# Maxima by a repeated column, one group of norm products for W_out, and a new written-out order in a fused attention and MLP kernel

## The chip, the cores and the metric

One core of one Trainium2 chip runs the kernel. The metric is the device time of the whole program in microseconds, the median of several runs. Five engines run beside each other, each through its own queue in order: TensorE (PE in the profile, its weight loads PEld), VectorE (DVE), ScalarE (ACT), GpSimd (POOL), and SyncE (SP), which here issues nearly all DMAs.

## What is computed

```python
a = softmax(phi, axis=memory slots)                 # (8, 8, 576, 32)
k_m = einsum('bhsm,bhsd->bhmd', a, k); v_m = ...v   # 32 pooled keys and values a head
attn = softmax(q @ k_m^T / 8)                        # (8, 8, 576, 32)
x = (attn @ v_m), heads side by side                 # 4608 tokens x 512
h = x @ w_in                                         # 4608 x 2048
out = (h - tanh(h)) @ w_out                          # 4608 x 512, float32
```

The weights come as float64 and are read as pairs of 32-bit words. The kernel has a fast path for small h, which replaces h − tanh(h) by a polynomial; it is valid while the norms of v_m, of W_in's columns and of W_out's columns lie in windows that the kernel checks at run time. If the check failed, a second, general path would follow.

## The kernel before, in words

**Tiling and stages.** There are 8 batches (b) of attention and 18 units (u) of 256 tokens for the MLP, each unit in four blocks (fb) of 512 hidden columns. x is never formed: for each batch and block, P multiplies v_m by W_in (line 573), and the first product of the MLP, H (line 620), multiplies that by the attention weights. Every float32 operand that enters a product is split in a float16 high half and a low half, so a product is three.

**The order is written by hand.** `ORDER` (lines 71 to 133) is a list of words; `go` takes them one at a time, and each calls one step for the numbers behind it. A step that yields is continued by the next word of the same name: `H0.0 … H0.0` are the product and, later, its first reading on ACT. A trailing `x` turns around which PSUM place the step takes. `in_order` then chains all instructions of an engine in the order of the words, so the words fix the order on each engine (and in SP's DMA queue), while the engines wait for each other by data and by buffers alone. The words that matter here:

- `i…:tag`, `o…:tag`, `k…:tag`: SP loads a block of W_in, of W_out, or a block again for the check.
- `Z`: two warm-up products whose result nobody uses (line 856).
- `T`: float64 to float32 in three DVE steps (447, 450, 453), then ACT writes the high half (464). `L`, `Lv`, `Lp`: the low half by ACT and POOL (487, 489), by DVE (475), or by PE and ACT (481, 482, 484).
- `FX`, `FQ`: load the logits with tokens along the free axis. `X`: maxima of the logits over the tokens' axis of that layout (line 230 for batches 0 and 1, where they become the bias of an exponential, `YX`, line 235, and `XT`, `XU` turn the result on PE, 244 and 255, with copies 247 and 259; line 191 for the others). `XP`: the maxima of the other six batches, spread to all partitions by PE (202). `Y`, `YM`: subtract them; `YE`: exponential.
- `KA`, `KB`, `KR`: load k and v. `V`: pooling products (271, 279). `N`: divide (284, 285, 288). `U`, `UV`: turn and split the pooled k and v (311, 315, 545, 547).
- `Q`, `QT`: load q. `S`: scores (323) and their 32x32 transposes on DVE (332). `AM`, `AE`, `AD`, `AT`, `AS`: maximum, exponential, division, transposes back and split; their second halves run on POOL, or with a `v` on DVE.
- `P`: line 573, then a copy (586); `PL`, `PLp`: its low half on DVE (591) or by PE and ACT.
- `H`: line 620, then ACT squares it (627). `a`, `ap`: the polynomial on DVE, ACT, DVE (640, 642, 644). `g`, `c`/`cv`: high half on ACT (664), low half on POOL or DVE (670). `f`, `s`/`sv`: sums of blocks of it for a seven-product scheme (678 to 680), split on ACT (687) and POOL or DVE (691). `M`: the second product (748, or 767 for units 4 and later). `E`, `Ev`: the result is put together on DVE (806, 808, 817) and on POOL or, with a `v`, on DVE (810, 812), and stored.
- `SI`, `SO`: squares of W_in, W_out on ACT; `SS`, `SSv`: sums of them on POOL or DVE (508); `NI`, `NO`: column norms by products with a vector of ones (514, 529). `CW`, `CWv`: a window check of a weight block on ACT or DVE (498). `GG`, `GX`, `WD`: the verdict.

**The maxima before the change.** `top` takes the maximum per partition (two values), DVE multiplies them into two 128x128 diagonals (line 193), and `top_all` multiplies the 128x128 ones by these 256 columns in float32 (202), so that every partition has all 256 maxima.

**The norms of W_out before the change.** For each of four parts of four blocks: `SO` squares, `SS` sums four blocks to one 128x512 tile, `NO` makes four one-column products (529), ACT copies the four results (531); after the last part DVE sums the four parts (535).

Of the kernel before, what the change touches and what calls it, by code (L numbers as in the profile page):

```python
# [79 lines left out]
g2.0 M2.0 i12:kv2 T12 T12 T12 Y2 a2.1 CW1 H3.0 c2.0 T12 a2.1 Lv4 o11:gg T13 T13 P0.2 P0.2 M2.0 a2.1 H3.1 i14:kv3 g2.1 KA2 c2.1 ap3.0 FA3 PL0.2 YE2  # L80
Lv12 ap3.0 ap3.0 V2.0 V2.1 T6 P1.2x T13 M2.1 H3.1 M2.1 T6 T6 T13 g3.0 a3.1 N2 U2x P1.2 Lv13 PL1.2 a3.1 OP2 T6 OP2 UV2 T7 T7 T7 H0.2x H0.2 a3.1 g3.1 T7
Lv6 H1.2 H1.2 M3.0 c3.0 M3.0 a0.2 Lv7 ap1.2 a0.2 a0.2 P0.3 o12:kv2 T14 ap1.2 o14:kv3 Q2.1 BS0 U2 c3.1 g0.2 M3.1 M3.1 c0.2 P0.3 PL0.3 H1.3x ap1.2 T15
OP3 OP3 UV2 H0.3 T15 g1.2 H1.3 FQ3 c1.2 T15 H0.3 M0.2 T15 L15 a1.3 a1.3 S2.1 T14 T14 T14 S2.0x a0.3 a0.3 S2.1 S2.0 P1.3x P1.3 a1.3 g1.3 a0.3 P2.0 g0.3
AMv2.0 PL1.3 M0.2 L14 c1.3 c0.3 H2.2 H2.2 AMv2.0 AM2.1 AM2.1 a2.2 AE2.0 ADv2.0 P2.0 a2.2 H2.3 H2.3 a2.3 M1.2 M1.2 PL2.0 a2.2 BF0 g2.2 cv2.2 H3.2 L15
P2.1 H3.2 L14 M1.3 a2.3 a2.3 BH0 BL0 M1.3 ADv2.0 W2 AT2.0 ap3.2 P2.1 R1 O1 O1 AE2.1 ap3.2 ap3.2 PL2.1 BS1 BF1 AS2.0 AS2.0 M0.3 M0.3 H4.0 H4.0 ap4.0 R0
P2.2 H3.3 g2.3 c2.3 O0 O0 BH1 BL1 AD2.1 AD2.1 ap4.0 ap4.0 M2.2 R2 X3 g3.2 c3.2 P2.2 PL2.2 H3.3 H4.1 H4.1 ap3.3 ap3.3 g4.0 ap4.1 ap4.1 KR3.0 XP3 Y3
f4.0 s4.0 M2.2 QT3.0 ap3.3 g3.3 s4.0 YE3 cv4.0 M2.3 M2.3 H4.2 O2 O2 c3.3 ap4.1 AT2.1 R3 H4.2 BS2 P2.3 AS2.1 P2.3 g4.1 AS2.1 V3.0x PL2.3 ap4.2 ap4.2
BF2 BH2 M3.2 f4.1 ap4.2 f4.2 M3.2 H4.3x s4.1 KR3.1 s4.1 BL2 V3.1 N3 k4:q XX M3.3 M3.3 H4.3 ap4.3 ap4.3 g4.2 U3x U3 UV3 M4.0 M4.0 cv4.1 UV3 S3.0x ap4.3
O3 O3 P3.0 M4.0 M4.0 S3.0 AMv3.0 P3.0 M4.1 H5.0 BS3 AMv3.0 AE3.0 f4.3 k0:e g4.3 cv4.3 M4.1 M4.1 M4.1 PL3.0 c4.2 s4.2 s4.2 P3.1 H5.0 a5.0 a5.0 M4.2
sv4.3 H5.1 CW4 BF3 a5.0 BH3 BL3 H5.1 g5.0 k2:q c5.0 M4.2 M4.2 f5.0 QT3.1 M4.2 H5.2 s5.0 sv4.3 M4.3 P3.1 a5.1 ADv3.0 a5.1 M4.3 M4.3 PL3.1 S3.1 ADv3.0  # L90
s5.0 a5.1 AT3.0 M4.3 H5.2 S3.1 E4 g5.1 a5.2 a5.2 E4 CW2 f5.1 E4 E4 sv5.1 P3.2 M4.3 H5.3 H5.3 FQ4 M5.0 FA4 M5.0 a5.2 cv5.1 E4 E4 AS3.0 a5.3 sv5.1 M5.0
M5.0 CW0 AS3.0 H6.0 M5.1 M5.1 M5.1 M5.1 f5.2 a5.3 g5.2 KR4.0 cv5.2 s5.2 s5.2 a5.3 H6.0 a6.0 f5.3 a6.0 a6.0 P3.2 H6.1 s5.3 H6.1 f6.0 M5.2 M5.2 M5.2
M5.2 P3.3 g5.3 c5.3 s5.3 M5.3 ap6.1 ap6.1 PL3.2 H6.2 ap6.1 g6.1 P3.3 AM3.1 AM3.1 c6.1 AE3.1 X4 XP4 g6.0 M5.3 c6.0 s6.0 PL3.3 f6.1 H6.2 a6.2 KR4.1 M5.3
Ev5 Ev5 M5.3 s6.0 Ev5 Ev5 Ev5 a6.2 ADv3.1 ADv3.1 YM4 M5.3 s6.1 Ev5 a6.2 YM4 YE4 H6.3 H6.3 s6.1 QT4.0 AT3.1 ap6.3 ap6.3 M6.0 M6.0 AS3.1 AS3.1 g6.2 k3:e
f6.2 M6.0 sv6.2 V4.0 M6.1 M6.1 ap6.3 g6.3 f6.3 M6.0 M6.1 M6.1 sv6.3 sv6.2 H7.0 H7.0 a7.0 c6.2 V4.1 N4 W3 a7.0 sv6.3 M6.2 SI0 H7.1 a7.0 f7.0 H7.1 a7.1
U4 UV4 FQ5 UV4 M6.2 QT4.1 M6.2 a7.1 M6.2 U4 H7.2 H7.2 SSv0 NI0 a7.1 f7.1 a7.2 c6.3 M6.3 NI0 g7.0 a7.2 a7.2 s7.0 S4.0 c7.0 S4.0 AMv4.0 M6.3 M6.3 E6
s7.0 g7.2 c7.2 H7.3 H7.3 E6 a7.3 M6.3 E6 s7.1 E6 E6 W4 g7.1 M6.3 E6 s7.1 P4.0 P4.0 S4.1x S4.1 AMv4.1 a7.3 X5 CW3 AMv4.0 AE4.0 a7.3 g7.3 M7.0 M7.0 M7.0
M7.0 H8.0 H8.0 f7.2 c7.1 M7.1 M7.1 M7.1 M7.1 s7.2 f7.3 PL4.0 ap8.0 ap8.0 AMv4.1 AD4.0 ap8.0 XP5 s7.2 k5:e sv7.3 CW5 cv7.3 M7.2 KR5.0 AD4.0 f8.0 g8.0
M7.2 M7.2 M7.2 sv7.3 AE4.1 ADv4.1 s8.0 s8.0 c8.0 AT4.0 H8.1 YM5 ADv4.1 H8.1 P4.1 P4.1 M7.3 M7.3 a8.1 a8.1 a8.1 H8.2 AS4.0 PL4.1 M7.3 Ev7 H8.2 a8.2 FA5
QT5.0 YM5 a8.2 YE5 f8.1 M7.3 Ev7 P4.2 P4.2 g8.1 M7.3 AS4.0 c8.1 s8.1 s8.1 Ev7 Ev7 a8.2 g8.2 Ev7 H8.3 M8.0 Ev7 M8.0 c8.2 M8.0 V5.0 M8.1 AT4.1 AS4.1  # L100
KR5.1 PL4.2 H9.0 H8.3 a8.3 a8.3 a8.3 H9.0 f8.2 a9.0 a9.0 s8.2 s8.2 M8.1 M8.1 V5.1 f8.3 P4.3x P4.3 N5 s8.3 k6:e M8.0 M8.1 g8.3 H9.1x H9.1 a9.0 PL4.3
U5x s8.3 UV5 ap9.1 f9.0 M8.2 M8.2 UV5 ap9.1 ap9.1 c8.3 f9.1 M8.2 M8.2 M8.3 g9.0 c9.0 M8.3 SI1 k7:q SS1 U5 S5.0 g9.1 M8.3 sv9.0 k8:e E8 E8 H9.2 E8 E8
S5.0 M8.3 M8.3 AS4.1 H9.2 H9.3x sv9.0 CW6 ap9.2 ap9.2 ap9.2 QT5.1 c9.1 M9.0 M9.0 M9.0 E8 E8 s9.1 s9.1 AM5.0 H9.3 a9.3 AM5.0 f9.2 a9.3 FQ6 a9.3 NI1x
NI1 AE5.0 AD5.0 AD5.0 H10.0x H10.0 M9.1 M9.1 a10.0 s9.2 P5.0 f9.3 S5.1x a10.0 g9.2 P5.0 c9.2 a10.0 M9.0 M9.1 H10.1 s9.2 CW8 M9.1 M9.2 g9.3 c9.3 S5.1
AMv5.1 AMv5.1 AE5.1 M9.2 M9.2 M9.2 AT5.0 AS5.0 X6 XP6 s9.3 H10.1 s9.3 M9.3 PL5.0 ap10.1 H10.2 AS5.0 ADv5.1 ap10.1 ap10.1 g10.1 f10.1 g10.0 YM6 f10.0
H10.2 a10.2 FA6 P5.1 P5.1 c10.0 CW7 YM6 PL5.1 M9.3 a10.2 a10.2 QT6.0 M9.3 M9.3 M9.3 s10.0 E9 E9 s10.1 H10.3x KR6.0 H10.3 H11.0 cv10.1 a10.3 E9 E9 E9
E9 a10.3 a10.3 YE6 P5.2 P5.2 s10.0 M10.0 M10.0 M10.0 KR6.1 V6.0 H11.0 PL5.2 a11.0 H11.1 k10:q a11.0 s10.1 f10.2 s10.2 M10.0 M10.1 g10.2 a11.0 H11.1
ap11.1 f10.3 s10.2 ap11.1 M10.1 M10.1 ap11.1 f11.1 c10.2 M10.2 V6.1 N6 g10.3 c10.3 sv10.3 sv10.3 H11.2 SI2 SSv2 U6 UV6 U6 UV6 H11.2 a11.2 M10.2 M10.2
S6.0 QT6.1 ADv5.1 P5.3x a11.2 AT5.1 f11.0 P5.3 AS5.1 S6.0 M10.1 AM6.0 s11.1 PL5.3 AS5.1 a11.2 M10.3 M10.3 M10.3 E10 AM6.0 M10.3 s11.0 NI2 NI2 AE6.0
k9:e CWv9 s11.0 g11.0 E10 E10 H11.3 H11.3 E10 E10 AD6.0 g11.1 ap11.3 ap11.3 ap11.3 c11.0 g11.2 M10.2 M10.3 E10 H12.0x H12.0 a12.0 AD6.0 M11.0 c11.1  # L110
FQ7 AT6.0 a12.0 M11.0 M11.0 s11.1 M11.1 S6.1x c11.2 f11.2 S6.1 P6.0 M11.0 M11.1 M11.1 M11.1 k11:e f11.3 CW10 P6.0 PL6.0 X7 s11.2 s11.2 AS6.0 KR7.0
g11.3 c11.3 H12.1 P6.1 P6.1 a12.0 f12.0 H12.1 a12.1 s11.3 s11.3 M11.2 M11.2 M11.2 a12.1 PL6.1 a12.1 f12.1 M11.2 s12.0 g12.0 c12.0 H12.2 AS6.0 XP7 YM7
H12.2 a12.2 s12.0 M11.3 M11.3 M11.3 M11.3 FA7 a12.2 H12.3 g12.1 c12.1 Ev11 Ev11 H12.3 CWv11 a12.2 AM6.1 a12.3 a12.3 KR7.1 AM6.1 YM7 M12.0 Ev11 Ev11
Ev11 P6.2 a12.3 M11.3 H13.0 s12.1 s12.1 M12.0 M12.0 Ev11 M12.0 P6.2 PL6.2 g12.2 c12.2 H13.0 ap13.0 H13.1x M12.1 AE6.1 AD6.1 W5 ap13.0 ap13.0 M12.1
f12.2 QT7.0 M12.1 H13.1 YE7 a13.1 f13.0 sv12.2 sv12.2 g12.3 cv12.3 W6 a13.1 a13.1 V7.0 f12.3 H13.2 AD6.1 AT6.1 M12.2 M12.2 M12.2 QT7.1 M12.1 M12.2
# [1023 lines left out]
```

## Time and profile before

| | |
|---|---|
| median of 3 runs | 635.2 us (635.11 to 636.61) |
| the profiled execution | 635.34 us, span 633.1 us |
| granted TensorE clock | 0.998 |
| DMA | 85.03 MB, mean 134 GB/s |

The span is the time from the first to the last instruction of the profiled execution; what lies around it belongs to the time too. The profile's engines are busy in the sense of start to end of an instruction. Products on PE are pipelined: a product's listed duration holds its flight through the array, so the time from the start of one product to the start of the next is shorter than that duration, and it is the former that adds up.

### The profile page before, as it was taken

The page shows a single profiled execution, that of the slowest core. Times are in us where ns is not written, and L with a number is a line of the kernel's source. Part 1 is how long each engine was busy: PE and PEld are TensorE (multiplying, and loading weights), DVE is VectorE, ACT ScalarE, POOL GpSimd, SP SyncE. Part 2 cuts the span into 40 slices and gives each one's busy share as a digit, 9 for nine tenths or more (in the row PEclk, how much of TensorE's full clock was granted, in tenths as well). Part 3 has the DMA queues.
Part 4 walks back from the last instruction along what each step waited for, and adds up shares of the span by engine and source line. Part 5 has one row for each costly group of instructions (what it writes and reads, how often), then busy time and mean ns, then how long its engine had stood idle before and what let it go on. Part 6 is the DMA issues. An engine that isn't in the chain of part 4 may idle for free.

```text
span 633.1 us, 16291 instructions
## 1 busy us (share of the span) xinstructions
PE 618.6 (98%) x6908; PEld 485.4 (77%) x6908; DVE 570.4 (90%) x763; ACT 428.5 (68%) x601; POOL 350.7 (55%) x314
## 2 busy tenths in 40 slices
PE   8789999999999999999999999999999999999996
...
GB/s 342 415 290 281 245 248 179 97 73 68 188 136 159 51 75 66 64 163 120 108 96 110 120 60 154 105 88 173 38 38 172 119 102 84 50 152 35 167 100 39
DMA packets 25872, 85.03 MB, mean 134 GB/s; under 512 B 2752, under 2 KB 2752, under 8 KB 25024
## 3 DMA queue, kind: packets, MB, share of 16 engines
...
q8 instruction: 56, 0.92, 0.6%
...
HBM read 72.37 MB, written 11.53 MB: 133 GB/s over the span
## 4 chain that ended last, share of the span: by engine, by line
PE 83%; DVE 9%; DMA 4%; ACT 2%; issue 1%; SPq 0%; DVEq 0%; ACTq 0%
PE h L620 26%; PE x L767 22%; PE o L767 16%; PE o L748 7%; PE o1h L748 3%; PE pp L573 3%; DMA q<-in_qt_dram 2%; PE pkv L271 2%; DMA raw<-in_w_in_dram 2%; PE psc L323 1%; DVE h L640 1%; DVE h L644 1%; DVE bw L707 1%; DVE bw L700 1%; DVE s L678 1%
## 5 line engine op out<-in xcount | busy, mean ns | idle before, releaser
L620 PEld LDWEIGHTS <-ph 128*128 128x128 f16 x2304 | 178.2, 98 | 19.7 <-issue 4.0
L670 POOL TENSOR_TENSOR g<-h,g 128x512 f16<-128x512 f32 x114 | 128.3, 1147 | 100.1 <-ACT g L664 89.9
L691 POOL TENSOR_TENSOR f<-s,f 128x512 f16<-128x512 f32 x86 | 107.4, 1269 | 86.0 <-ACT f L687 81.1
L767 PEld LDWEIGHTS <-f 128*128 128x128 f16 x1344 | 129.2, 98 | 20.8 <-issue 5.2
L620 PE MATMUL h<-ah,ph 128*128 128x256 f16 (+3 forms) x1536 | 138.6, 246 | 0.7 <-DVE h L640 0.7
L767 PE MATMUL x<-bt,f 128*128 128x256 f16 x1008 | 128.3, 273 | 0.0
L642 ACT ACTIVATE u<-u,beta 128x1024 f32<-128x1024 f32 x72 | 82.5, 1146 | 46.7 <-DVE h L640 46.5
L767 PEld LDWEIGHTS <-g 128*128 128x128 f16 x1008 | 97.9, 98 | 14.7 <-issue 3.5
L627 ACT ACTIVATE u<-h 128x1024 f32<-128x1024 f32 x72 | 73.3, 1019 | 47.4 <-PE h L620 31.4
L640 DVE SCALAR_TENSOR_TENSOR h<-h,u 128x1024 f32<-128x1024 f32 x72 | 87.9, 1221 | 19.4 <-ACT u L627 17.9
L644 DVE SCALAR_TENSOR_TENSOR h<-u,h 128x1024 f32<-128x1024 f32 x72 | 92.7, 1289 | 11.7 <-ACT u L642 11.4
L664 ACT ACTIVATE g<-h 128x512 f16<-128x512 f32 (+2 forms) x128 | 68.2, 580 | 20.0 <-DVE h L644 13.4
L620 PE MATMUL h<-al,ph 128*128 128x256 f16 (+3 forms) x768 | 75.1, 246 | 0.0
L748 PEld LDWEIGHTS <-g 128*128 128x128 f16 x384 | 36.7, 98 | 45.2 <-issue 3.0
L687 ACT ACTIVATE f<-s 128x1024 f16<-128x1024 f32 x56 | 58.6, 1048 | 11.1 <-DVE s L680 7.0
L748 PE MATMUL o<-wout_hi,g 128*128 128x512 f16 x192 | 59.0, 379 | 0.0
L678 DVE TENSOR_TENSOR s<-h 128x512 f32<-128x512 f32 x56 | 45.3, 809 | 2.0 <-DVE h L644 0.5
L767 PE MATMUL o<-wout_hi,f 128*128 128x256 f16 x224 | 45.9, 273 | 0.0
L767 PE MATMUL o<-wout_hi,g 128*128 128x256 f16 x224 | 45.8, 273 | 0.0
L767 PE MATMUL x<-wout_hi,g 128*128 128x256 f16 x224 | 45.8, 273 | 0.0
L767 PE MATMUL o<-bt,g 128*128 128x256 f16 x336 | 45.3, 273 | 0.0
L586 ACT ACTIVATE ph<-pp 128x1024 f16<-128x1024 f32 x32 | 32.4, 1014 | 17.6 <-PE pp L573 16.7
...
## 6 DMA issues: line engine op xcount, KB each, us to landing
...
```

The lines of the kernel that those rows point to most:

```text
L620: nc.tensor.matmul(hp[:, k, tu : tu + w], st[b]["p"][fb][i][:, g, cs], st[b][ax][:, g, ta : ta + w], start=(n == 0 and k % 2 == 0 and m == ...
L627: nc.scalar.activation(uu, hp, AF.Square, scale=1.0 / (S_A * S_P))
L640: nc.vector.scalar_tensor_tensor(t, hp, C2 * S_G / (S_A * S_P), uu, op0=ALU.mult, op1=ALU.mult)
L642: nc.scalar.activation(uu, uu, AF.Square, bias=c["beta"])
L644: nc.vector.scalar_tensor_tensor(h3, uu, CC, t, op0=ALU.add, op1=ALU.mult)
L664: nc.scalar.activation(hi, x, AF.Copy)
L670: eng.tensor_tensor(lo[:, ks], x[:, ks], hi[:, ks], op=ALU.subtract)
L678: nc.vector.tensor_tensor(s[:, 0:2], pair, a_block(h3, 0, 0).unsqueeze(1).to_broadcast((P, 2, 2, P)), op=ALU.add)
L687: nc.scalar.activation(f[:, 0], s, AF.Copy)
L691: eng.tensor_tensor(f[:, 1, ks], s[:, ks], f[:, 0, ks], op=ALU.subtract)
L748: nc.tensor.matmul(o, gx[:, k, P * tt : P * tt + P], wx[:, 4 * fb + k, :], start=(first and k == 0 and wx is wout_hi and gx is gh), stop=( ...
L767: nc.tensor.matmul(dst, a(na, kk), b(nb, kk), start=(new and kk == 0 and na == 0 and nb == 0), stop=(end and kk == 1 and na == 1))
```

## The change

Three things. **One:** DVE no longer builds diagonals. PE takes the column of maxima, repeated 128 times by a stride of zero, as its stationary operand, and the identity as the moving one, once for each of the two columns. **Two:** the four parts' squares of W_out are added up in one float16 tile `wn` on POOL or DVE, and one group of four products and one copy on ACT follow; the window of that check is a little narrower. **Three:** `ORDER` is new. It has 1703 words for 1710 before: the words of the three norm groups are gone, and some steps go to another engine (`E` for `Ev` in units 5, 7, 11 and 14, `Lv2` for `L2`, and so on).

```diff
-WO_WIN = (1.002 * 2.0 ** -6, 3.493)
+WO_WIN = (1.004 * 2.0 ** -6, 3.486)
...
-        dg = big.tile([P, 2, P], F32, tag="qt", name=f"dg{b}", bufs=1)
-        nc.vector.tensor_tensor(
-            dg, self.c["ident"].unsqueeze(1).to_broadcast((P, 2, P)),
-            mx.unsqueeze(2).to_broadcast((P, 2, P)), op=ALU.mult,
-        )
-        d["dg"] = dg
+        d["mx"] = mx
...
-        nc.tensor.matmul(pa[:, 0, 0:256], self.c["ones"], dg.rearrange("p a b -> p (a b)"), start=True, stop=True)
+        for r in range(2):
+            row = d["mx"][:, r : r + 1].to_broadcast((P, P))
+            nc.tensor.matmul(pa[:, 0, P * r : P * r + P], row, self.c["ident"], start=True, stop=True)
...
     def squares_sum(i, eng=nc.gpsimd):
...
+        steps = [(0, 2), (1, 3)] if eng is nc.gpsimd else [(slice(0, 2), slice(2, 4))]
+        for k, m in steps:
             eng.tensor_tensor(sq[:, k], sq[:, k], sq[:, m], op=ALU.add)
+        if ("n", i) in acc:
+            if i == 0:
+                acc["n"] = big.tile([P, 512], F16, tag="wn", name="wn", bufs=1)
+            to = acc["n"] if i == 0 else sq[:, 0]
+            eng.tensor_tensor(to, sq[:, 0], sq[:, 1], op=ALU.add)
+            if i > 0:
+                eng.tensor_tensor(acc["n"], acc["n"], sq[:, 0], op=ALU.add)
+        else:
+            eng.tensor_tensor(sq[:, 0], sq[:, 0], sq[:, 1], op=ALU.add)
...
     def norms_out(part):
...
-            nc.tensor.matmul(pa[:, 0, k : k + 1], sq[:, 0, P * k : P * k + P], c["ones16"], start=True, stop=True)
-        yield
-        nc.scalar.activation(acc["n"][:, :, part], pa[:, 0, 0:4], AF.Copy, scale=(S_W * S_Q) ** -2)
-        yield
-        if part == 3:
-            o = N_CHECK - 4
-            nc.vector.tensor_reduce(stat[:, o : o + 4], acc["n"], axis=AX.X, op=ALU.add)
+            nc.tensor.matmul(pa[:, 0, k : k + 1], acc["n"][:, P * k : P * k + P], c["ones16"], start=True, stop=True)
+        yield
+        nc.scalar.activation(stat[:, N_CHECK - 4 : N_CHECK], pa[:, 0, 0:4], AF.Copy, scale=(S_W * S_Q) ** -2)
```

The start of the order, up to the first pooling of batch 1 (`V1.0`):

```diff
-Z0.0 i0:gg i1:gg T0 T0 T0 T0 Z0.0 Z0.0 Z0.0 Z0.0 Z0.0 i6:kv3 T3 T3 T3 Z0.0 Z0.0 Z0.0 Z0.0 Z0.0 FX0 T3 Z0.0 Z0.0 Z0.0 Z0.0 Z0.0 X0 Lp0 Lp0 YX0 Z0.0
-Z0.0 Lp3 Lp3 Z0.0 XT0 i2:gg i3:pp5 T1 T1 T1 i4:kv2 T1 XT0 XU0x T2 KA0 XU0 Z0.0 T2 T2 V0.0 Z0.0 Z0.0 Lv1 KB0 V0.1 N0 T2 L2 L2 U0x UV0 o2:gg Z0.0 Z0.0
-o3:gg Z0.0 T9 T9 T9 U0 Q0.0 S0.0x S0.0 Q0.1 S0.1 UV0 KA1 P0.0x P0.0 P0.1 PLp0.0 AM0.0 AM0.0 AE0.0 P0.1 PLp0.1 o4:gg o5:pp2 S0.1 AM0.1 AM0.1 AD0.0
-AD0.0 AE0.1 AD0.1 W0 AT0.0 T10 T9 AD0.1 AT0.1 PLp0.1 AS0.0 Q1.0 AS0.0 PLp0.0 Lp9 H0.0x ASv0.1 T10 ASv0.1 H1.0 Lp9 T10 T10 L10 o6:gg o7:gg H1.1 H0.0
-T11 T11 FX1 X1 o1:gg YX1 a0.0 o0:pp2 L10 H1.0 XT1 Z0.0 T11 T8 T8 T8 XT1 XU1 XU1 a1.0 a0.0 KB1 V1.0 a0.0 V1.1 T8 Lv8 a1.0 g0.0 H1.1 c0.0 N1 T11 L11
+i1:gg Z0.0 Z0.0 Z0.0 Z0.0 Z0.0 Z0.0 Z0.0 Z0.0 Z0.0 Z0.0 Z0.0 Z0.0 Z0.0 Z0.0 Z0.0 i0:gg T0 T0 FX0 X0 YX0 XT0x T0 T0 i6:kv3 T3 i2:gg i3:pp5 Lp0 Z0.0 T3
+T3 XT0 Z0.0 Z0.0 i4:kv2 T1 T3 Lp3x KA0 Lp3 XU0x XU0 V0.0 T1 T1 T2 KB0 T1 T2 T2 Lp0 o2:gg Lv1 o3:gg T2 Lv2 Z0.0 Z0.0 Z0.0 Z0.0 V0.1 N0 U0x T9 T9 T9 UV0
+Z0.0 Z0.0 Z0.0 U0 Q0.0 S0.0x S0.0 Q0.1 S0.1 T9 UV0 P0.0x P0.0 o5:pp2 o4:gg AM0.0 AM0.0 AE0.0 P0.1x P0.1 S0.1 AM0.1 o6:gg AM0.1 AE0.1 AD0.0 W0 PLp0.0
+PLp0.0 AD0.1 AD0.0 AT0.0 T10 PLp0.1 PLp0.1 AD0.1 AT0.1 o7:gg T10 Q1.1 Lp9 KA1 AS0.0 ASv0.1 AS0.0 H0.0x FX1 Lp9 H0.0 T10 ASv0.1 H1.0 T11 T11 T10 L10
+H1.0 L10 X1 o1:gg o0:pp2 H1.1 YX1 XT1 XU1 KB1 Z0.0 a0.0 a0.0 XT1 XU1 o9:pp4 T11 T11 T8 T8 T8 T8 a1.0 a1.0 o10:pp5 a0.0 L11 V1.0 g0.0 c0.0 V1.1 N1 Lv8
...
```

More of the change, by code (lines that the diff above doesn't have):

```diff
@@ L80 @@
[L80 to L115, printed above, removed]
```

84 lines of the change are left out of this document (58 added, 26 removed).

## The prediction

> **What bounds the kernel now.** I read the page first: span, engines, slices, chain.
>
> ```profile
> span 633.1 us, 16291 instructions
> ...
> PE 618.6 (98%) x6908; PEld 485.4 (77%) x6908; DVE 570.4 (90%) x763; ACT 428.5 (68%) x601; POOL 350.7 (55%) x314
> ...
> PE   8789999999999999999999999999999999999996
> ...
> PE 83%; DVE 9%; DMA 4%; ACT 2%; issue 1%; SPq 0%; DVEq 0%; ACTq 0%
> ```
>
> TensorE (PE) has 98% of the span and 83% of the chain that ended last. Its slices are full but for the first three and the last. So I asked for four stretches: up to the first k/v pooling of batch 0 (V0.0), up to that of batch 1 (V1.0), the body, and the tail.
>
> ```profile
> 0.00:19.40 19.40, 16.09 (x62) 7.28 (x62) 14.10 (x22) 8.94 (x11) 1.20 (x16) 1.00 0.92 357
> 19.40:48.00 28.60, 23.52 (x326) 14.81 (x330) 25.43 (x46) 18.47 (x28) 10.28 (x7) 1.00 0.89 345
> 48.00:628.00 580.00, 578.77 (x6528) 463.35 (x6520) 530.41 (x696) 401.06 (x563) 339.23 (x291) 1.00 0.34 117
> 628.00:633.10 5.10, 0.26 (x3) 0.00 (x0) 0.42 (x1) 0.00 (x0) 0.00 (x0) 0.73 0.33 116
> ```
>
> The columns after the length are the busy time of PE, its weight loads, DVE, ACT and POOL, then the clock, the DMA share and GB/s. In the body PE is idle for 580.00 − 578.77 = 1.23 us, and the view of its waits there has these two:
>
> ```profile
> PE h L620 <- DVE h L640: 0.7, 1, 0.7
> PE pkv L271 <- issue: 0.4, 1, 0.4
> ```
>
> This decides how the new order must be read. DVE at 530.41 of 580 us, ACT and POOL may be emptied or filled: while PE is never without work, that is worth nothing beyond the 1.23 us. What can shorten the kernel is PE work removed, or an earlier moment at which PE goes over to unbroken work (V1.0, 47.66). What can lengthen it is a later such moment, dearer PE work, or new waits in the body. The tail holds the last eviction and its store, in the same order after the change.
>
> **Part 1, the start of the order.** These rows of the timeline carry it:
>
> ```profile
> 6.33 0.43 DVE L447 TENSOR_SCALAR wt<-raw 128x512 uint32<-128x512 uint32 x1 [0.82 <-DMA raw<-in_w_in_dram]
> 6.67 1.28 DVE L450 SCALAR_TENSOR_TENSOR wt<-raw,wt 128x512 uint32<-128x512 uint32 x2
> 9.08 0.69 DVE L447 TENSOR_SCALAR wt<-raws 128x1024 uint32<-128x1024 uint32 x1
> 9.20 1.06 ACT L464 ACTIVATE win_hi<-wt 128x1024 f16<-128x1024 f32 x1 [7.18 <-DVE wt L453]
> 9.80 1.23 DVE L450 SCALAR_TENSOR_TENSOR wt<-raws,wt 128x1024 uint32<-128x1024 uint32 x1
> 10.71 1.02 PE L481 MATMUL pw<-wt,idw 128*128 128x512 f32 x2
> 12.20 1.35 DVE L230 TENSOR_REDUCE mx<-pt 128x2 f32<-128x1152 f32 x1
> 12.86 1.03 PE L856 MATMUL warm<-nid 128*128 128x512 f16 x4
> 13.29 1.00 ACT L484 ACTIVATE win_lo<-pw 128x1024 f16<-128x1024 f32 x1
> 14.19 1.43 ACT L235 ACTIVATE pt<-pt,mx 128x576 f32<-128x576 f32 x2
> 18.84 0.54 ACT L259 ACTIVATE e<-pkv 64x128 f32<-64x128 f32 x2
> 19.44 1.10 PE L271 MATMUL pkv<-kv,e 128*32 128x129 f32 x32 [1.42 <-ACT e L259]
> 20.47 1.04 PE L856 MATMUL warm<-nid 128*128 128x512 f16 x4
> 21.43 1.09 PE L271 MATMUL pkv<-kv,e 128*32 128x129 f32 x32
> 23.09 0.16 DVE L284 TENSOR_SCALAR kr<-pkv 128x2 f32<-128x2 f32 x1 [2.20 <-PE pkv L279]
> 23.89 0.87 DVE L447 TENSOR_SCALAR wt<-raw 128x512 uint32<-128x512 uint32 x2
> 26.35 0.72 PE L323 MATMUL psc<-q,kT 64*32 64x288 f32 x16 [0.70 <-DMA q<-in_qt_dram]
> 27.16 0.78 DVE L332 STREAM_TRANSPOSE sc<-psc 128x576 f32<-128x576 f32 x1
> 41.56 1.34 DVE L230 TENSOR_REDUCE mx<-pt 128x2 f32<-128x1152 f32 x1
> 47.66 1.98 PE L271 MATMUL pkv<-kv,e 128*32 128x129 f32 x64 [0.64 <-ACT e L259]
> ```
>
> Block i1 now lands first, so T0's first step waits for i0, at 6.33. Its L450 pair (1.28) ends near 8.3. X0, moved up, reduces for 1.35, to 9.6; its logits are the third transfer instead of the fourth. YX0's two exponentials (1.43) hold ACT to 11.1, and T0's conversion (1.06) stands behind them, to 12.1. PE then makes Lp0's product (2.15 us from the row at 10.71 to the next at 12.86), three warm words (0.43 each: two words fill 12.86 to 13.72), and Lp3's product from 15.6 to 17.7. T3's conversion doesn't hold that up: behind X0 come 1.28 + 0.69 + 1.23 and once more 1.23 on DVE and 1.06 on ACT, to 15.1. On ACT, Lp3's copy (1.00) is now ahead of XU0's two (0.54): they end at 19.5, and V0.0, which waits for them, starts at 19.5 instead of 19.44. Four steps were reordered, and nothing is won.
>
> Between V0.0 and V0.1 stand four warm words now, two before. Two words cost 21.43 − 20.47 = 0.96 with the switch to V0.1, so V0.1 starts at 19.5 + 1.03 + 1.83 = 22.36, which is **0.9 us later**. Queued behind it: N0 on DVE waits for V0.1 (23.09, behind 2.20 us of idleness; Lv2, which was POOL's and ACT's L2, goes into that gap). Behind N0 stand T9's three steps, from 23.89 right up to the transposes of S0.0 at 27.16. The q transfer that releases S0.0 at 26.35 doesn't move, so S0.0 stays, but its transposes slide to about 28.1. From there to X1 (41.56) DVE has the same steps as before, nearly without a gap, and X1 releases YX1, XT1, XU1 and V1.0 one after another. So V1.0 goes from 47.66 to 48.6, with the same PE work done ahead of it. T9's conversion, moved up on ACT, and H0.0's square, ahead of T10's, lie in ACT gaps; the order of the later loads changes, but FX1 still waits for AT0.1. Bounds: 0, if DVE catches up on the way (of its idle 28.60 − 25.43 = 3.17 us in that stretch, 2.20 lie ahead of N0, and 0.97 after it or elsewhere), to 1.9, if Lp9, which now waits for PLp0.0's copy on ACT, adds one copy (1.00) that lasts past V1.0. I take **+0.9**: what is left of DVE's idle time is waits for POOL and ACT inside the very chain that slides.
>
> **Part 2, the products.**
>
> ```profile
> L529 PE MATMUL pno<-ones,sqo 128*128 128x1 f16 x16 | 1.0, 165 | 0.0
> L202 PE MATMUL pmx<-dg,ones 128*128 128x256 f32 x12 | 3.7, 394 | 0.0
> L202 PEld LDWEIGHTS pmx<-dg,ones 128*128 128x128 f32 x12 | 1.8, 191 | 0.0
> L244 PE MATMUL pet<-ident,pt 128*128 128x128 f32 x16 | 2.3, 278 | 0.8 <-ACT pt L235 0.8
> L244 PEld LDWEIGHTS pet<-ident,pt 128*128 128x128 f32 x16 | 1.8, 140 | 1.4 <-ACT pt L235 1.2
> L193 DVE TENSOR_TENSOR dg<-ident,mx 128x256 f32<-128x256 f32 x6 | 3.4, 573 | 0.2
> ```
>
> Norms: four groups of four take 1.0 us, 0.25 each from first start to last end. The flight of the last (0.165) lies under what follows, which leaves 0.09. Three groups go: **−0.3**. The three evictions and the reduction that go are ACT's and DVE's, off the path. The added sums, one more on POOL or DVE for each later part, delay only NO3, which the check at the very end waits for.
>
> Maxima: six products of one 256-column stream in two passes (12 records) become six pairs of 128 columns (24 records). One of the old took 3.7 / 6 − 0.394 = 0.22 between its two starts, 0.44 in all. Four passes of half the columns are 0.44 again if the stream sets the pace, as it does in the transposes: 1.04 us for eight less their flight is 0.11 each, although their loads are listed at 140 ns. If the load of a two-pass fp32 product (191 ns, the row of the product that is replaced) sets the pace, a pair takes 0.76, that is +0.33, and six +2.0. Below nothing it can't go, the columns being as many. Nearest is the transposes' row, of the same shape, but its loads are shorter; I take 0.1 each, **+0.6**. The 573 ns that DVE saves are no PE time.
>
> [...]
>
> **Part 3, the moved steps of the body.** Net, DVE gives four evictions' adds to POOL, and three windows to ACT; it takes four of the attention's splits, three of the low halves of g and one of f, and loses the six L193 products. All of that lies beside PE's 578.77 us. The steps that stand just in time before a product are about as many as before, and each such place can become a wait. Bounds: −1.2, if both old waits go, to about +4, if the body's start became as loose as the stretch before it (28.60 − 23.52 = 5.1 us idle). I take 0, nearest to the body's own row.
>
> Sum on the profiled execution (635.34 us, span 633.1 and 2.2 around it): +0.9 − 0.3 + 0.6 + 0 = +1.2, so 636.5. It ran 0.14 above the median of 635.2; by the median I forecast **636.4**. A difference under 0.3% (1.9 us) counts as none, since that is about what a measurement here can tell.
>
> **Rivals.**
> *Hidden anyway* (12%): DVE catches up the 0.9 us before X1, and the maxima stream like transposes. Only −0.3 stays: 634.9. For it: the 0.97 us of idle DVE. Against: waits inside a chain slide with it.
> *The maxima's loads set the pace* (14%): 635.2 + 0.9 − 0.3 + 2.0 = 637.8, slower. It decides from 0.22 us a product on (1.3 us for six). For it: 191 ns against a stream of 0.11; against: 140 against 0.11 did no harm.
> *New waits in the body* (17%): some 2 to 4 us where just-in-time steps come late, 638.4 to 640.4. For it: 1.23 us of waiting leaves far more room to get worse than better. Against: DVE's sum is smaller.
> *A shorter start* (12%): the T9 conversion (1.06) that leaves ACT's queue ahead of PLp0.1 brings V1.0 forward by as much, and the body loses its waits: 635.2 − 1.06 − 0.3 − 1.23 = 632.6, faster. Against: X1's chain on DVE, not ACT, ends last there.
>
> **How the numbers follow.** The forecast has 45%. Some 5% of it lies over 637.1, so slower is 14 + 17 + 5 = 36%, same 40 + 12 = 52%, faster 12%. The range leaves out the shorter start and the upper end of the new waits: 633.7 to 639.6.
>
> **What would show it.** V1.0 near 48.6 in the timeline, V0.1 near 22.4 and the S0.0 transposes near 28.1 show part 1 right; V1.0 at 47.7 or sooner refutes it. Part 2: the pairs of maxima between 0.44 and 0.76 us from start to the next work, and one group of norms at L529's successor. Part 3: PE idle between V1.0 and the tail near 1.2 us. If it is over 3 us, or V1.0 comes a microsecond sooner, the forecast is wrong.

## The result and the profile after

The changed kernel takes **640.18 us** (median of 4 runs, 639.89 to 640.76), the kernel before 635.51 beside it: 1.0072 times as long, interval 1.006 to 1.0084. The forecast was 636.4, its range ended at 639.6. The page of the profiled execution (640.17 us):

```profile
span 638.1 us, 16280 instructions
...
PE 620.1 (97%) x6908; PEld 486.2 (76%) x6908; DVE 565.4 (89%) x756; ACT 433.3 (68%) x607; POOL 348.1 (55%) x313
...
PE   8789999999999999999999999999999999999995
...
PE 71%; DVE 19%; ACT 5%; issue 2%; POOL 2%; DMA 0%; SPq 0%; DVEq 0%; POOLq 0%; ACTq 0%
```

PE's slices look as before; the chain does not: DVE had 9% of it and has 19% now, although DVE is busy for 5.0 us less. The four stretches, cut where V0.0, V1.0 and the tail begin:

```profile
0.00:19.40 19.40, 16.13 (x59) 7.18 (x59) 13.03 (x21) 7.25 (x10) 1.20 (x16) 1.00 0.91 350
19.40:48.20 28.80, 23.98 (x319) 14.64 (x320) 27.25 (x47) 20.28 (x30) 8.18 (x6) 1.00 0.91 350
48.20:630.80 582.60, 579.71 (x6531) 464.35 (x6532) 524.72 (x689) 405.79 (x569) 338.75 (x291) 1.00 0.34 116
630.80:638.10 7.30, 0.27 (x3) 0.00 (x0) 0.42 (x1) 0.00 (x0) 0.00 (x0) 0.83 0.24 84
```

PE's idle time in the body is 582.60 − 579.71 = 2.89 us (1.23 before), the tail 7.30 us (5.10 before), V1.0 at 48.2 (47.66 before). The view of PE's waits in the body (engine, line, what it waited for; us in all, times, longest) had two rows before; now:

```profile
PE pp L573 <- DVE ph L591: 0.8, 1, 0.8
PE pp L573 <- DVE h L640: 0.4, 1, 0.4
PE pkv L268 <- ACT e L223: 0.4, 1, 0.4
PE pkv L268 <- PE h L620: 0.4, 1, 0.4
PE pp L573 <- DVE h L644: 0.3, 1, 0.3
PE h L620 <- DVE ph L591: 0.3, 1, 0.3
```

Four of the six, 1.8 of 2.6 us, are waits for a place in PSUM that DVE (the cubic's L640 and L644, the low halves' L591) has not yet read out. For V7.0 and V3.0 (`pkv`) the view names another engine, but both start 0.10 us behind the end of a step of the cubic on DVE (473.23 and 179.35). The view counts from the modelled end of a product's flight. Counted from start to start against what the same word takes elsewhere in the trace, nine words lose 4.42 us: P4.2 0.96, P5.2 0.60, P3.0 0.55, V7.0 0.55, V3.0 0.52, H5.1 0.44, P3.2 0.34, H5.0 0.26, H6.0 0.20. Before it was three: H5.2 0.84, V5.0 0.58, P5.2 0.30, in all 1.72.

In the start, the timeline shows V0.0, V0.1, N0, S0.0's transposes, X1 and V1.0:

```profile
19.39 1.09 PE L268 MATMUL pkv<-kv,e 128*32 128x129 f32 x32 [1.33 <-ACT e L256]
...
22.25 0.82 PEld L268 LDWEIGHTS pkv<-kv,e 128*32 128x32 f32 x32 [0.42 <-issue]
...
23.83 0.16 DVE L281 TENSOR_SCALAR kr<-pkv 128x2 f32<-128x2 f32 x1 [0.16 <-PE pkv L276]
...
27.71 0.77 DVE L329 STREAM_TRANSPOSE sc<-psc 128x576 f32<-128x576 f32 x1
...
42.11 1.33 DVE L227 TENSOR_REDUCE mx<-pt 128x2 f32<-128x1152 f32 x1
...
48.19 1.07 PE L268 MATMUL pkv<-kv,e 128*32 128x129 f32 x29 [0.21 <-ACT e L256]
```

So the span's 5.0 us are: start +0.53, V1.0 to the first product of the last word (M17.3) 582.06 in place of 579.78 (+2.28), last product to the end +2.19 (the tails go by the span as printed and are good to 0.05 us). In what follows "start" is V1.0, "body" and "tail" are these two lengths (the last word's six products between take 0.55).

My theory then: the order makes the body's waits, the tail is a code effect, the start is little. Rivals: the new products or sums cost the time; the tail belongs to the stores or the last words' order; the waits are local and can be filled.

### The profile page after: what moved, and what is told of

It is laid out like the page before. It is cut to its first block, busy times and chain, and to the rows that moved or that the text cites. A ratio compares the mean times of both kernels' runs of the same rounds, so it can differ in the third digit from the quotient of the medians.

```text
span 638.1 us, 16280 instructions
## 1 busy us (share of the span) xinstructions
PE 620.1 (97%) x6908; PEld 486.2 (76%) x6908; DVE 565.4 (89%) x756; ACT 433.3 (68%) x607; POOL 348.1 (55%) x313
## 4 chain that ended last, share of the span: by engine, by line
PE 71%; DVE 19%; ACT 5%; issue 2%; POOL 2%; DMA 0%; SPq 0%; DVEq 0%; POOLq 0%; ACTq 0%
PE h L620 21%; PE x L767 18%; PE o L767 14%; PE o L748 5%; DVE h L640 3%; DVE h L644 2%; PE pp L573 2%; PE pkv L268 2%; PE warm L856 2%; PE o1h L748 2%; DVE bw L707 1%; DVE ph L591 1%; DVE bw L700 1%; PE psc L320 1%; DVE s L678 1%
## 5 line engine op out<-in xcount | busy, mean ns | idle before, releaser
L670 POOL TENSOR_TENSOR g<-h,g 128x512 f16<-128x512 f32 x108 | 127.0, 1198 | 81.0 <-ACT g L664 76.7
L691 POOL TENSOR_TENSOR f<-s,f 128x512 f16<-128x512 f32 x84 | 102.8, 1244 | 93.8 <-ACT f L687 65.7
L644 DVE SCALAR_TENSOR_TENSOR h<-u,h 128x1024 f32<-128x1024 f32 x72 | 90.0, 1250 | 17.7 <-ACT u L642 14.6
L640 DVE SCALAR_TENSOR_TENSOR h<-h,u 128x1024 f32<-128x1024 f32 x72 | 87.7, 1220 | 15.1 <-ACT u L627 13.5
L678 DVE TENSOR_TENSOR s<-h 128x512 f32<-128x512 f32 x56 | 45.5, 812 | 1.6
L591 DVE SCALAR_TENSOR_TENSOR ph<-pp,ph 128x1024 f16<-128x1024 f32 x30 | 36.3, 1212 | 2.9 <-ACT ph L586 2.9
```

The lines of the kernel that those rows point to most:

```text
L640: nc.vector.scalar_tensor_tensor(t, hp, C2 * S_G / (S_A * S_P), uu, op0=ALU.mult, op1=ALU.mult)
L644: nc.vector.scalar_tensor_tensor(h3, uu, CC, t, op0=ALU.add, op1=ALU.mult)
L670: eng.tensor_tensor(lo[:, ks], x[:, ks], hi[:, ks], op=ALU.subtract)
L678: nc.vector.tensor_tensor(s[:, 0:2], pair, a_block(h3, 0, 0).unsqueeze(1).to_broadcast((P, 2, 2, P)), op=ALU.add)
L691: eng.tensor_tensor(f[:, 1, ks], s[:, ks], f[:, 0, ks], op=ALU.subtract)
```

## The experiments

All stages by the profile (span, V1.0, body, tail in us; time is the median, or the one run where there was one):

| run | span | V1.0 | body | tail | time | ratio to before, interval |
|---|---|---|---|---|---|---|
| before | 633.1 | 47.66 | 579.78 | 5.11 | 635.5 to 635.8 | |
| after | 638.1 | 48.19 | 582.06 | 7.30 | 640.18 | 1.0072 (1.006 to 1.0084) |
| e1_old_order | 635.8 | 48.26 | 581.83 | 5.17 | 637.11 | 1.0019 (1.001 to 1.0028) |
| e2_pad | 635.9 | 48.09 | 582.07 | 5.19 | 638.18 | 1.0039 (1.0025 to 1.0053) |
| e3_pad_before | 636.1 | 48.20 | 580.01 | 7.34 | 637.89 | 1.0035 (1.0021 to 1.0048) |
| e4_quarter | 643.7 | 47.69 | 588.0 | 7.5 | 645.8, one run | |
| e5_old_engines | 723.6 | 47.73 | 669.84 | 5.48 | 725.62 | 1.1419 (1.1402 to 1.1436) |
| e6_six_moved | 637.6 | 47.83 | 582.27 | 6.96 | 640.40 | 1.0073 (1.006 to 1.0087) |
| e8_two_warm | 638.1 | 48.10 | 582.15 | 7.30 | 640.20, one run | |
| e9_att4 | 639.8 | 48.24 | 583.36 | 7.65 | 641.99, one run | |
| e10_sum_later | 638.2 | 47.52 | 584.99 | 5.15 | 638.36 | 1.0041 (1.0027 to 1.0055) |
| e11_half_step | 634.6 | 48.12 | 580.32 | 5.61 | 636.96, one run | |
| e12_sum_idle | 636.1 | 47.68 | 582.69 | 5.18 | 638.24 | 1.0048 (1.0035 to 1.0062) |
| e13_fewer_warm | 636.5 | 47.63 | 583.11 | 5.22 | 638.26 | 1.0042 (1.0029 to 1.0055) |
| f1_maxima_only | 633.0 | 47.60 | 579.64 | 5.22 | 635.42 | 0.9998 (0.9989 to 1.0007) |
| f3_maxima_moved | 632.5 | 48.00 | 578.79 | 5.16 | 634.75 | 0.9982 (0.9973 to 0.9991) |
| f4_half_act | 638.6 | 47.99 | 582.56 | 7.51 | 640.67, one run | |
| f5_half_both | 634.2 | 48.31 | 579.73 | 5.61 | 636.70, one run | |

**The tail: e2_pad and e3_pad_before.** In both kernels ScalarE issues the last store, then branches over the second path. Before, its first instruction behind the branch is at 632.26 and the next at 632.34; after, the first is at 634.96 and the next only at 637.23, and every other engine waits for it at the closing barrier. In the trace, 769 instructions stand ahead of that branch in ScalarE's queue before and 782 after, so the code behind it lies elsewhere. That its place is what counts is the "code theory". The edit, with 4 copies in the changed kernel and 12 in the one before:

```diff
+    gap = const.tile([P, 1], F32, name="gap")
+    for _ in range(4):
+        nc.scalar.activation(gap, c["one"], AF.Copy)
     with ExitStack() as inner:
         split_path(inner, tc, c, ins, out)
```

> The changed kernel with four copies of one column added on ScalarE ahead of its first work, so that the code behind its last branch lies four instructions later. If the 2.2 us more in the tail are a wait for one more block of ScalarE's code: last product to end of span falls from 7.3 to about 5.1 and the time from 640.2 to 638.0, with no other stage moved by more than 0.2. If they belong to the stores or to the order of the last words: 640.2, tail 7.3.

> The kernel before with twelve such copies on ScalarE, which puts the code behind its last branch where the changed kernel has it. If the place of the code is what counts: the tail grows from 5.1 to about 7.3 and the time from 635.5 to 637.7. If it belongs to the changed order: 635.5, tail 5.1.

Both came as the code theory had it: 7.30 fell to 5.19, and 5.11 grew to 7.34; 638.18 and 637.89 us. All 18 profiles fit: the tail is 6.96 to 7.65 us in the seven runs where 781 or 782 instructions stand ahead of the branch, and 5.1 to 5.6 us where there are 766 to 777, or 786 (e2). In e6, with 781, the wait stands one instruction further on (634.86 to 637.23). In e11 and f5 there are 777, so their tails of 5.61 us are part of what they gain below.

In the trace ScalarE's branch is at 632.04 and the first instruction behind it at 634.96, 2.9 us later (629.23 and 632.26 before, 3.0). What the second wait, 2.2 us more, is for stays open. That it is a wait for one more block of code, the "if" of e2's expectation, is not shown: of the 8 KB packets of code (`instruction` among the profile's DMA queues) behind the last store, the sixth is over at 635.93 and the seventh begins at 637.87, when the wait is past.

**The code in the old order: e1_old_order, f1_maxima_only.** The order of before, less the words of three norm groups; then the kernel before with the maxima's edit alone.

> Both changes of the code (maxima as two products of a repeated column, one group of norm products) in the order of before; the three groups of norm words go. If the new order is what costs the time: 635.5 - 0.3 = 635.2 us, V1.0 within 0.2 of 47.7, six words of maxima at 0.44 each, last product to end of span about 5.1. If the pairs of maxima cost what the prediction took (0.1 each): 635.8. If the code is what costs the time (waits that follow from the products): 638 or more.

> The kernel before with the change of the maxima alone. If the pairs stream at 0.44 us and the six products that DVE loses (0.57 each) shorten the wait at V5.0 (0.58 to about 0.25): 635.6 - 0.3 = 635.3 us. If the pairs cost 0.1 each as the prediction took: 636.2. If the maxima cost the 1.4 us that the kernel with both changes in the old order lost: 637.

The six pairs take 0.44 to 0.53 us to the next product, the single products took 0.43 to 0.52: the maxima cost nothing. f1 is level with before (0.9998), with V5.0's wait down from 0.58 to 0.25 and one of 0.25 at V7.0 that was not there; so the 2.2 us between the bodies of f1 and e1 (1.3 to 1.7 us between their times) are the norms' change. e1 itself, 637.11, lies between what was expected of the order and of the code: its body, 581.83, is nearly as long as the changed kernel's 582.06, but its waits lie elsewhere. In e1 four words between 528 and 560 us lose 2.5 us, 1.49 of them before M15.0. The timeline there, in the kernel before and in e1, DVE's rows first and then GpSimd's, has the last of the sums (L508; L513), the forms of window 15.1 (L678 to L680) and GpSimd's step beside them:

```profile
548.20 1.14 DVE L508 TENSOR_TENSOR sqo<-sqo 128x1024 f16<-128x1024 f16 x2
549.25 0.68 DVE L678 TENSOR_TENSOR s<-h 128x512 f32<-128x512 f32 x1
549.97 0.43 DVE L679 TENSOR_TENSOR s<-s,h 128x256 f32<-128x256 f32 x1
550.43 0.42 DVE L680 TENSOR_TENSOR s<-s,h 128x256 f32<-128x256 f32 x1
...
550.65 1.34 POOL L564 TENSOR_TENSOR al<-af,ah 128x576 f16<-128x576 f32 x1 [2.61 <-ACT ah L562]
```

```profile
550.28 0.42 DVE L513 TENSOR_TENSOR wn<-wn,sqo 128x512 f16<-128x512 f16 x1
550.62 0.68 DVE L678 TENSOR_TENSOR s<-h 128x512 f32<-128x512 f32 x1
551.34 0.42 DVE L679 TENSOR_TENSOR s<-s,h 128x256 f32<-128x256 f32 x1
551.80 1.39 DVE L680 TENSOR_TENSOR s<-s,h 128x256 f32<-128x256 f32 x1
...
553.56 0.42 DVE L808 SCALAR_TENSOR_TENSOR r<-x,r 128x256 f32<-128x256 f32 x1
...
551.56 1.35 POOL L564 TENSOR_TENSOR al<-af,ah 128x576 f16<-128x576 f32 x1 [2.61 <-ACT ah L562]
```

One added step of 0.42 us puts L680 behind the start of GpSimd's L564 in place of ahead of it, and L680 takes 1.39 in place of 0.42: it ends 0.28 us behind GpSimd's step. L808, two steps further on in DVE's queue, then ends at 553.98, and M15.0, which by the view of waits waited for it, starts at 554.13:

```profile
PE x L767 <- DVE r L808: 1.3, 1, 1.3
```

**The same sum elsewhere: e10_sum_later, e12_sum_idle, e13_fewer_warm.**

From e1's order, `SSv2` moves from behind `k24:q` to behind the third `a15.2` (e10) or behind `f15.2` (e12, e13), and e13 also drops three of the first sixteen `Z0.0`. For e12:

```diff
-k24:q SSv2 M14.3 M14.3 AS7.1
+k24:q M14.3 M14.3 AS7.1
...
-f15.2 s15.2 a15.3
+f15.2 SSv2 s15.2 a15.3
```

> The order of before with both changes of the code, the third sum of W_out's squares (DVE) moved behind the last step of window 15.2. If the added 0.42 us step, put ahead of window 15.1, made M14.1 to M15.0 wait in the kernel with the old order: the 2.5 us lost there go, 637.1 - 2.5 = 634.6 us, under the kernel before by the three groups of norm products (0.3) and part of the wait at V5.0. If the sums cost as much wherever they stand: 637.

> The order of before with both changes of the code, the third sum of W_out's squares moved to where GpSimd is idle for 3 us (behind the step f15.2). If its steps on DVE are short (0.68, 0.42, 0.42) only while GpSimd is idle, the 2.5 us lost at M14.1 to M15.0 mostly go: 634.6 to 635.2 us, the kernel before at 635.75. If any place in that stretch is too full for 1.5 us more: 637 or more.

> As e12, without three of the sixteen warm words that stand ahead of PE's first real product (they compute nothing that is used). Where the full clock is granted late (7.4 us), that product waits for the warm words until 11.5 us, but its operand is there at 10.3: if so, V0.0 comes at 19.0 to 19.5 whatever the moment, V1.0 at 47.5 to 47.7, 0.3 to 0.6 us less than e12. If the start hangs on the transfers instead: as e12.

Both places failed: 638.36 and 638.24. The profiled execution of e10, 640.08, is the slowest of its five: behind a wait of 3.25 us for DVE's L817, which stands behind the long sums, the clock was granted at half for 3.41 us, so its body of 584.99 lies some 1.7 us above what the median stands for. The durations are as e12 expected, though. The three steps in e10, beside a busy GpSimd, and in e12, beside an idle one:

```profile
553.90 1.64 DVE L506 TENSOR_TENSOR sqo<-sqo 128x1024 f16<-128x1024 f16 x1
555.57 1.26 DVE L511 TENSOR_TENSOR sqo<-sqo 128x512 f16<-128x512 f16 x1
556.87 1.26 DVE L513 TENSOR_TENSOR wn<-wn,sqo 128x512 f16<-128x512 f16 x1
```

```profile
559.34 0.68 DVE L506 TENSOR_TENSOR sqo<-sqo 128x1024 f16<-128x1024 f16 x1
560.06 0.43 DVE L511 TENSOR_TENSOR sqo<-sqo 128x512 f16<-128x512 f16 x1
560.52 0.43 DVE L513 TENSOR_TENSOR wn<-wn,sqo 128x512 f16<-128x512 f16 x1
```

The three take 4.2 us beside the busy GpSimd and 1.5 beside the idle one. In e12 the waits of 1.49 and 0.40 us from M15.0 on are gone (those of 0.38 and 0.26 before it stay), but the short sums push DVE's next steps into GpSimd's (DVE's L644 begins at 560.86, GpSimd's L691 at 560.93), and H16.1, NO3 and H16.2 lose 2.1 us. Neither place had room for 1.5 us on DVE. e13 brought V0.0 to 19.18 us, but V1.0 stays at 47.63 (47.68 in e12) and H0.1 and U1 wait 0.5 us more: nothing won.

**The start: e8_two_warm.** `Lv2 Z Z Z Z V0.1 N0` becomes `Lv2 Z Z V0.1 Z Z N0`.

> The changed kernel with two of the four warm words between V0.0 and V0.1 put behind V0.1. As the prediction has it: V0.1 comes about 0.9 sooner after V0.0 (2.86 falls to 2.0) and the S0.0 transposes and V1.0 follow by about as much, V1.0 minus V0.0 from 28.8 to about 28. If other waits between (Lp9, XU1) take it up: V1.0 minus V0.0 stays within 0.2 of 28.8.

V0.1 comes 2.03 us behind V0.0 (2.86 in after), yet V1.0 stays at 48.10, now 29.12 us behind V0.0, which neither expectation had. DVE's rows in e8:

```profile
23.98 0.41 DVE L444 TENSOR_SCALAR wt<-raw 128x512 uint32<-128x512 uint32 x1
24.83 0.43 DVE L444 TENSOR_SCALAR wt<-raw 128x512 uint32<-128x512 uint32 x1 [0.44 <-DMA raw<-in_w_out_dram]
...
27.61 0.77 DVE L329 STREAM_TRANSPOSE sc<-psc 128x576 f32<-128x576 f32 x1
```

Here T9's second step waits for its transfer until 24.83, so the transposes are at 27.61 (27.71 in after). In after, DVE waits 0.16 us for V0.1's result and not for the transfer. So in this one execution the transfer takes what the two words gave.

Something else differs from profile to profile, whatever the order: the moment at which PE gets its full clock. PE's warm words begin at 1.94 in all runs, a product every 0.43 us until the full clock is granted and every 0.22 from then on. The stretch 4.90 to 7.90 (PE's products in brackets) in before, e1 and after:

```profile
4.90:7.90 3.00, 3.00 (x13) 1.27 (x12) 2.00 (x5) 0.00 (x0) 0.00 (x0) 1.00 1.02 414
```

```profile
4.90:7.90 3.00, 3.00 (x10) 1.15 (x9) 1.97 (x4) 0.00 (x0) 0.00 (x0) 1.00 1.03 416
```

```profile
4.90:7.90 3.00, 3.00 (x9) 1.15 (x8) 1.98 (x5) 0.25 (x1) 0.00 (x0) 1.00 1.02 404
```

The clock's column says 1.00 throughout, since the records begin with the first grant; the number of products tells the rate. By these records full rate begins at 5.73, 7.37 and 7.62. In the old order the first real products stand behind these words: V0.0 is at 19.44 and 20.26, V1.0 at 47.66 and 48.26, with the same words. The profile of before had an early moment, that of after a late one. At like moments (7.3 to 7.5) V1.0 is at 48.20 and 48.26 in the old order (e3, e1) and at 48.09 and 48.12 in the new (e2, e11); at 5.0 to 6.2, it is at 47.5 to 47.7 in the old and at 47.7 in the new (e4, e5), but at 48.3 in f5, where T9's second step waits for its transfer as in e8. So at like moments the two starts differ by some 0.1 us. The chain of part 1 is there all the same: in 16 of the 18 profiles V1.0 stands 25.9 to 26.4 us behind V0.1 (26.23 before, 25.94 after, 26.00 in e3), and the other two are e8 (27.09) and f5 (26.58).

**The maxima: e4_quarter.** Each pair cut into eight products of 32 columns.

```diff
-    nc.tensor.matmul(pa[:, 0, P * r : P * r + P], row, self.c["ident"], start=True, stop=True)
+    for q in range(0, P, 32):
+        nc.tensor.matmul(pa[:, 0, P * r + q : P * r + q + 32], row, self.c["ident"][:, q : q + 32], start=True, stop=True)
```

> The changed kernel with each pair of maxima cut into eight products of 32 columns (16 passes, each with its own load of the repeated column), the same columns in all. If the stream sets the pace: a word of maxima stays at 0.44 us. If each load of 0.19 us sets it: 16 x 0.19 = 3.0 us a word. If a load takes PE for the 0.11 us that 128 columns stream: 16 x 0.11 = 1.75.

```profile
L200 PE MATMUL pmx<-ident,mx 128*128 128x32 f32 x96 | 11.4, 272 | 0.0
L200 PEld LDWEIGHTS pmx<-ident,mx 128*128 128x128 f32 x96 | 11.3, 190 | 0.2
```

A word takes 1.70 to 1.79 us to the next product. Its sixteen passes start (11.4 / 6 − 0.272) / 15 = 0.109 us apart although every load is listed at 190 ns: in this run a pass with its float32 load takes PE 0.109 us, and the rest of the load's listed time lies beside other passes. A pass of the pairs, with 128 columns, takes no longer (0.44 us for four, 0.11 each; the old ones, with 256 columns, took 0.22), so there the loads add nothing.

**The body: e6_six_moved.** Six waiting words are moved behind the next ready product, for instance:

```diff
-M7.3 P4.2 s8.0 H8.2 M7.3 M7.3 c8.0
+M7.3 s8.0 H8.2 M7.3 M7.3 P4.2 c8.0
-V7.0 M12.1 a13.1
+M12.1 V7.0 a13.1
```

> The changed kernel with six words moved behind the next ready product (V3.0x, H5.1x, P3.2, P4.2, P5.2, V7.0), which lost 3.4 us between them waiting for a place in PSUM to be read out. If these waits are local: 640.2 - 3.4 = 636.8, at least 2.5 of it in the trace. If DVE sets the pace of the body and the waits come back at later words: within 1 us of 640.2.

The moved words wait no more, and the body is 582.27, no shorter (582.06 in after). The waits of e6:

```profile
PE h L620 <- DVE h L640: 1.9, 2, 0.9
PE pp L573 <- DVE h L644: 0.7, 1, 0.7
PE pkv L268 <- DVE ph L591: 0.4, 1, 0.4
PE x L767 <- DVE r L808: 0.2, 1, 0.2
```

H6.0 loses 1.10 now, H8.3 1.12, P3.0 0.96, V6.0 0.52. "The waits are local" falls: what reads PSUM out is late as a whole.

**Old engines, new places: e5_old_engines, e9_att4.** First every window's and softmax's step goes back to the engine it had before; then AD4.0 and AS4.0 alone, from DVE to GpSimd.

> The changed kernel, its words in the new order, but each window's and softmax's steps on the engine that they had before (some 60 groups of steps go back to their old engine). If the work moved between engines made the new waits of the body: V1.0 to the last product goes from 582.1 back to 580 or less, 638 us or less. If the places of the words made them: 582 still, 640 with a tail of 7.3, 638 with one of 5.1.

> The changed kernel with two softmax steps of block 4 (AD4.0 and AS4.0, which the new order gave to DVE) back on GpSimd, as before. They take DVE some 2 us ahead of P4.2, where PE lost 0.96 us waiting for PL4.1 to be read out. If DVE's queue is what made PL4.1 late: the wait at P4.2 falls below 0.3 and no other wait grows by more than 0.3 in 300 to 330 us. If the place of the words does: still 0.8 to 1.1.

e5 takes 725.62 us at a granted clock of 0.962, which neither theory had: places and engines in such an order are chosen together, and it tells the two apart no further. In e9 P4.2 no longer waits, so DVE's queue did hold PL4.1 up; but GpSimd has no room either:

```profile
PE h L620 <- POOL al L564: 1.3, 1, 1.3
PE x L767 <- POOL g L670: 0.9, 1, 0.9
```

M7.3 loses 1.06 and M8.1 1.47; the body grows to 583.36.

**Relieving DVE and ScalarE: e11_half_step, f4_half_act, f5_half_both.** The first edit is e11's, the second f4's, and f5 has both; each leaves out half of the columns of its step.

```diff
-        nc.vector.scalar_tensor_tensor(h3, uu, CC, t, op0=ALU.add, op1=ALU.mult)
+        ks = slice(None) if stay else slice(0, 2)
+        nc.vector.scalar_tensor_tensor(h3[:, ks], uu[:, ks], CC, t[:, ks], op0=ALU.add, op1=ALU.mult)
...
-        nc.scalar.activation(uu, uu, AF.Square, bias=c["beta"])                   
+        nc.scalar.activation(uu[:, 0:2], uu[:, 0:2], AF.Square, bias=c["beta"])
```

> The changed kernel with DVE's second step of the cubic (L644) on half its columns in the windows whose first step goes to SBUF: the last multiply-add of half these columns is left out. DVE has some 20 us less to do, the order, PE's work and the transfers stay. If the length of DVE's queue makes the new waits of the body: V1.0 to the last product falls from 582.1 to 580 or less and the nine waits of over 0.17 us from 4.4 us in all to under 2. If they hang on ACT, GpSimd or on where a word stands: 581.5 or more.

> The changed kernel with ScalarE's second square of the cubic (L642) on half its columns: the square of the other half is left out. ScalarE has some 35 us less to do. If the waits that stayed when DVE was relieved (V3.0x, P3.0, H5.0, H5.1x, P4.2, H8.3) hang on ScalarE: V1.0 to the last product falls from 582.1 to 581 or less. If they hang on DVE's order alone: 581.7 to 582.2.

> The changed kernel with both steps of the cubic halved, L644 on DVE as in the run before and L642 on ScalarE: half of either step is left out. If the two engines' queues account for all new waits: V1.0 to the last product 579.5 or less (before: 579.8, with 1.7 us of such waits; three groups of norms less). If a rest hangs on GpSimd or on the places of the words: 580 or more.

The body is 580.32 with DVE relieved, 582.56 with ScalarE relieved (above both expectations), 579.73 with both. So DVE's relief takes back 1.74 of the body's 2.28 us. It is not all: six waits (2.60 us) stayed in e11, and ScalarE's relief, worth nothing alone, takes another 0.6 once DVE is out of the way. V7.0's wait goes in e11 and stays in f4 (0.56), which speaks for DVE and against ScalarE, which the view named. With both relieved the body is as long as before the change, though 579.73 lies just above the 579.5 that was expected. That does not prove that the two queues made the whole rise, since the kernel before was not relieved in the same way and might have gained too. Which of the moved steps fills DVE's queue is not settled; e5, which was to tell, was too coarse.

**A faster version: f3_maxima_moved.** f1 with two words moved:

```diff
-M4.2 H5.2 s5.0 sv4.3 M4.3 P3.1
+M4.2 s5.0 sv4.3 M4.3 H5.2 P3.1
-M8.0 V5.0 M8.1 AT4.1
+M8.0 M8.1 V5.0 AT4.1
```

> As f1, with H5.2 moved behind M4.3 and V5.0 behind M8.1 (they wait 0.84 and some 0.25 us). If a wait goes when another ready product is put ahead of it: 635.3 - 1.1 = 634.2 us. If the reading out on DVE is late as a whole, as the six moved words showed, the waits come back at the next words: 635.0 to 635.6.

```profile
48.00:627.30 579.30, 579.03 (x6543) 464.01 (x6544) 529.57 (x691) 401.38 (x563) 339.41 (x291) 1.00 0.35 117
```

PE idles for 0.27 us in the body (1.23 before). 634.75 against 635.84 us beside it: 0.9982, interval 0.9973 to 0.9991, faster than both kernels. Here the moves pay, between the two expectations: H5.2 and V5.0 wait no more, but M4.3, which stands ahead of H5.2 now, loses 0.28.

## Why the prediction was wrong

- **Part 3 failed, and it is the mechanism, not a size.** "The steps that stand just in time before a product are about as many as before … I take 0": new waits of 2.7 us came (4.42 for 1.72), within the 2 to 4 us of the rival "new waits in the body" (17%). That 640.18 also lies in that rival's 638.4 to 640.4 is luck: without the tail's 2.2 us the kernel takes 638.18 (e2). Counting such places says nothing about how late their readers run. For five of the nine words that wait, the order of the list had turned round: V3.0, P3.0, H5.0, H6.0 and P5.2 stood behind the last reader of their place in the old list (ap4.1, ap4.3, S3.0, a5.3, a10.3) and stand ahead of it in the new one, which could have been read from the two orders. "Against: DVE's sum is smaller" was misread too: DVE is busy for 565.4 us in place of 570.4, and PE waits longer for it. How much of this comes from the moved steps and how much from the room made for the sums below stays open.
- **The tail failed.** "The tail holds the last eviction and its store, in the same order after the change" was true of PE, DVE and the stores and cost nothing there. Unseen was that more instructions on ScalarE move the code behind a branch: 2.2 us, nearly half of the rise, and shown in both directions (e2, e3). Why the wait arises at that place is not shown.
- **Part 1 was mis-sized**: +0.9 forecast, +0.53 in the profile, about 0.1 either way at like moments of the clock. The chain slid as described, and lost a third on the way: V0.1 is 0.82 later (22.25; 22.36 forecast), N0 0.74 (23.83), S0.0's transposes 0.55 (27.71, not 28.1), X1 0.55 (42.11), V1.0 0.53. Between N0 and the transposes lie 3.88 us in place of 4.07. Nor is the slide the new order's alone: the row that the forecast started from, V0.0 at 19.44, was that of an early full clock, and at a late one (e3) the old order has V0.0 at 20.21, V0.1 at 22.20 and V1.0 at 48.20. Lp9's wait, named as a bound, came (0.89 us from start to start).
- **Part 2, maxima**: +0.6 forecast, 0 measured. The listed 191 ns of a load were taken as a price; e4 has 0.109 us from start to start, so the rival "loads set the pace" was wrong.
- **Part 2, norms**: −0.3 as forecast for the products (each group takes 0.10 to 0.12 us to the next product, before and after). "The added sums, one more on POOL or DVE for each later part, delay only NO3" failed in the old order: words beside them lose 2.5 us there, against the 0.3 that the products give back. In the new order the last two run beside an idle GpSimd (0.68, 0.43 and 0.43 us each); what making that room cost elsewhere was not measured alone.

The terms as measured: start +0.5 in this pair of profiles, maxima 0, norms −0.3, new waits +2.6, tail +2.2, together the span's 5.0; the medians' difference is 4.67.
